# A product in the element order of the transpose that follows it, and a rewritten task order

## The chip, the core and the metric

The kernel runs on one core of a Trainium2 chip. The core has five instruction streams that run beside each other and wait for one another by semaphores: PE (TensorE, matrix products into PSUM), ACT (ScalarE), DVE (VectorE), POOL (GpSimd) and SP (SyncE, which here only issues transfers). The metric is the device time of one execution in microseconds; the median of the runs counts.

## The reference

The input x has 2048 positions and 640 channels. A conditioning vector c gives six modulation vectors. The first half of the block multiplies a shifted k with v, convolves the product along the whole sequence with a filter as long as the sequence, and multiplies by q. The second half is a two-layer MLP with a shift of channel groups between.

```python
mod = (silu(c) @ w_mod)                    # sa, ca, ga, sb, cb, gb
h = layernorm(x) * (1 + ca) + sa           # this is q of the first half
k_shift = sum(k_pad[:, t:t+S, :] * shift_k[:, ks-1-t] for t in range(4))
kv = k_shift * v
y = irfft(rfft(kv, 2*S) * rfft(ssm_k, 2*S))[:S] + kv * ssm_D
x = x + ga * (h * y)
h = layernorm(x) * (1 + cb) + sb
m = gelu(layernorm(h) @ w1)                # four channel groups shifted by 1, -1, 2, -2 positions
x1 = h + shift(m) @ w2
x = x + gb * (x1 + gelu(layernorm(x1) @ w3) @ w4)
```

Everything is bfloat16 outside of the accumulations.

## The kernel before

The Fourier transforms are products with cosine and sine matrices that the kernel makes itself. A position is n = 64 * n2 + n1, and a transform has two stages: stage 1 over n2 (32 values), stage 2 over n1 (64 values).

The channels are taken in five blocks of 128 partitions, b = 0 to 4. `sT`, `kT` and `vT` hold the filter, k and v with channels on partitions and positions along the free dimension; `dma_start_transpose` brings k and v in so. `kT` and `vT` share the buffer R5. For each block, `k_shift(b, s2)` makes half of the shifted k (1024 positions) with eight matmuls against diagonal matrices into a PSUM tile `ps_ksh` (line 457), and DVE multiplies the tile with v (line 462). `to_slots` (line 395) then lets DVE transpose the 2048 bf16 numbers of a partition as 1024 pairs (seen as int32) in squares of 32 by 32, into `kvL`, which is Rb. Its result has n2 on the partitions, which is what stage 1 contracts over. The filter goes the same way (`sL`, also in Rb, from Ra). `stage1` (line 408) puts its result into T01 through evacuations of PSUM by ACT (line 209) or DVE (line 211), and `stage2` (line 425) puts the spectra into R3 (filter, `KSX`) and R5 (product, `XS`, over kT and vT). Stage 2 takes its matrices `Gs` from RG. `inverse1` multiplies the spectra on DVE (line 606) and transforms back (lines 617 and 618), `inverse2` (line 658) finishes.

RH holds two of the three buffers for the early pieces of w_mod and after them the matrices of `inverse2`.

The MLP follows in sixteen tiles of 128 positions, in groups g: three single tiles first, then pairs. `chain_a` (lines 734 and 737) adds the first half to x, `chain_b` (748 or 752, then 753) modulates, `chain_c` (721 or 583) normalizes and turns the tile for the products `mm_w1` (815, 825), `mm_w2` (870), `mm_w3` (904) and `mm_w4` (934). Each chain ends in a layer norm: ACT squares and sums (726), `ln_finish` takes the mean on POOL or DVE (699 to 704) and the power -1/2 on POOL (709 to 714). `ln1_stats` (528 on DVE, or 536 and 537 on ACT) and `ln1_fin` (546 to 551, POOL) do the same for the first layer norm, which `make_q` (583 or 581, 590, 591) applies.

The order of the work is written out by hand in the string `ORDER`. Every call of `add` makes a numbered task with its reads and writes. A word of `ORDER` such as `121D` puts task 121 into the queue of DVE at that place; P is PE, A is ACT, G is POOL, S is SP, and the digits after a colon are the places (of four) in PSUM. A queue runs in this order, and a task waits there for its inputs. Some tasks may be given to either of two engines. The tasks that the text names:

| tasks | what |
|---|---|
| 32, 33; 45, 46 to 48 | negation of a part of Gs, and copies of it, first and second half |
| 116 to 135 | k_shift: matmuls (even) and product (odd), four to a block |
| 460 to 471 | first layer norm's statistics for tiles 8 to 15; 463 is tile 10, 464 tile 11, 467 tile 13 |
| 498, 502 to 511 | inverse2 for tiles 3 to 15 |
| 519, 520, 521, 522, 523 | tile 0, chain_a: two on DVE, the square, the mean, the power |
| 524, 525, 526, 527, 528, 529 | tile 0, chain_b and the normalization 529 |
| 540 to 549, 550 | tile 1, the same (543 and 544 end chain_a, 548 and 549 end chain_b) |
| 560 to 569, 570 | tile 2 |
| 588 to 595 | tiles 3 and 4, chain_a (594 and 595 end it) |
| 580, 581, 582 | first mm_w2, its sum and its square |

Of the kernel before, what the change touches and what calls it, by code (L numbers as in the profile page):

```python
# [10 lines left out]
I32 = mybir.dt.int32  # L11
ACT = mybir.ActivationFunctionType
ALU = mybir.AluOpType
PSUM = bass.MemoryType.PSUM

S, D, F = 2048, 640, 1728
P = 128
NT = S // P
ND = D // P
# [4 lines left out]
LFFT = 4096  # L24

ORDER = """
0S 19G 18D 20D 2S 27G 28D 31A 29D 30A 21G 23D 22D 4S 36G 37G 68G 69D 24A 25A 26G 84P:0 85A 3S 86P:1 87A 90P:2 91A 50G 72G 52D 73D 106P:3 107A 102P:0
104P:1 70G 71D 96P:2 6S 5S 88P:3 103D 74D 75D 8S 49G 118P:0 9S 119D 38G 105A 97A 39G 40A 89A 98P:1 99A 114P:2 1S 66D 10S 108P:3 115D 109A 92P:0 32G
67D 41G 93A 42G 43G 44A 54A 116P:1 11S 51D 53A 94P:2 112P:3 113A 117D 7S 122P:0 123D 80P:1 110P:3 111D 95A 81A 76P:2 77A 100P:0 101D 78P:1 82P:3 79A
33S 253D 34S 120P:2 121D 45G 46G 83A 178P:0 55G 179A 47S 184P:1 185A 35S 140P:3 141A 190P:0 191D 146P:1 147A 142P:2 143D 174P:3 175A 170P:0 182P:1  # L30
183A 171D 136P:2 137A 56G 200S 194P:3 144P:0 145A 195D 168P:1 48S 162P:2 163A 169D 148P:3 149D 192P:0 193A 196P:1 172P:2 173A 160P:3 161A 12S 57G 58G
197D 188P:0 189D 156P:1 152P:2 150P:3 176P:0 157A 151A 153D 177D 164P:1 138P:2 139D 165A 154P:3 155A 186P:0 187D 254D 158P:1 159A 180P:2 181A 260P:3
166P:0 167D 59G 60A 61G 201S 198P:1 261A 62G 63G 199D 124P:2 268P:3 203S 202S 211A 269A 13S 125D 14S 208A 65G 210D 15S 126P:0 266P:1 16S 270P:2 271A
128P:3 127D 264P:0 267A 265A 262P:2 263A 213D 214A 17S 130P:1 255D 276P:0 277A 129D 209D 219S 258P:2 259A 131D 134P:3 274P:0 275A 280P:1 281A 64A 135D
363G 278P:2 279A 132P:3 272P:0 273A 212G 220P:1 221A 256D 282P:2 283A 133D 222S 223P:3 224A 257D 288P:0 289A 284P:1 285D 292P:2 293A 286P:3 225S
294P:0 295A 290P:1 287D 291D 296P:2 297A 226P:3 227D 228S 229P:0 340P:1 230D 322P:2 231S 323D 341A 348P:3 349A 234S 480D 232P:0 249G 233D 326P:1 327A
243S 238S 360P:2 361D 356P:3 357A 328P:0 314P:1 250G 315A 358P:2 359A 329D 336P:3 306P:0 307A 318P:1 337D 320P:2 321A 319D 237G 483D 244S 330P:3 331A
352P:0 353D 242S 354P:1 355A 235P:2 386S 300P:3 236D 310P:0 311D 301A 246G 308P:1 239G 316P:2 317D 324P:3 309A 240S 350P:0 332P:1 312P:2 325A 251S
333A 313A 351D 298P:3 299D 247G 304P:0 305A 252G 344P:1 345D 241S 302P:2 303A 245G 338P:3 339D 342P:0 343A 334P:1 335D 346P:2 347A 364D 362S 365D
368P:3 486A 487D 369A 488D 248G 366P:0 216A 372D 370S 371G 367A 373D 374P:1 375A 376P:2 387G 481D 378S 377A 379G 380D 381D 442S 443P:3 382P:0 384P:1  # L40
385A 389D 388D 392P:2 394S 383A 393A 390P:1 391A 395G 397D 396D 398P:0 399A 402S 400P:2 401A 403G 405D 410S 411G 404D 408P:1 409A 406P:0 407A 413D
412D 416P:2 417A 420D 414P:1 415A 489A 418S 419G 421D 422P:0 423A 424P:2 425A 448S 449P:1 426S 427G 428D 450A 429D 430P:0 431A 432P:2 433A 436D 435G
434S 437D 438P:1 439A 440P:0 441A 490D 457S 458P:2 459A 454S 484D 444D 455P:3 479G 445S 456A 215G 495P:10 497A 217D 451S 452P:2 482D 492D 491D 218G
493D 453A 446P:3 485D 494D 496D 519D 532A 498P:01 499A 500A 501G 447D 511P:23 520D 522G 521A 513A 540D 560D 512A 541D 472S 502P:01 478G 505P:32 561D
524D 562A 473S 542A 591D 523G 525D 204S 526A 592D 593A 503A 504A 533D 588D 507A 563G 564G 543G 527D 565D 589D 590A 528G 529D 530P:0 531A 508P:12 566D
567A 545D 544G 546D 476S 477S 594G 595G 568D 548D 547A 535P:0 206S 553D 510A 600D 509A 596D 601D 597D 506A 536A 549G 550D 205S 602D 603A 551P:2 474S
537P:1 538A 475S 569G 570D 552D 571P:3 598D 534D 604G 572D 207S 599A 605G 558P:0 559A 556P:2 557A 554D 651D 578P:1 579A 555D 652D 576P:3 577A 653A
654D 609D 606D 607P:0 655D 656A 516S 467A 464D 610P:2 611D 580P:1 608D 620P:3 581D 582A 618P:2 621A 619A 657G 658G 663D 664D 665D 666A 659D 583G 584G
585D 586P:0 660D 661D 662A 514S 667D 587A 622P:1 461D 668G 669D 463A 623D 670S 625P:3 518G 636P:2 637A 671D 672S 624A 638P:0 639A 460D 462G 626D 627A
640P:1 641A 628D 629G 633D 630D 681P:2 682A 679P:3 680A 634P:0 642P:1 465G 643A 676D 677D 631P:2 635A 469D 632D 615A 616D 686P:3 687D 683P:1 617D 684D  # L50
466A 678D 703P:0 689G 515S 573A 697P:2 688A 699P:3 685A 704A 574D 575D 719D 690G 673D 720D 698A 785D 694A 695P:1 691D 692P:0 612A 693A 613D 614D 722D
721A 517S 644P:2 723D 700A 696A 724A 725G 769P:0 674D 765P:3 675D 786D 788D 789D 791D 645D 726G 727A 787A 701P:1 728D 766A 731D 729D 646D 770A 763P:2
468G 732D 733D 790A 702A 705P:30 730A 734A 792G 793D 647S 797D 735G 767P:1 851D 744A 852D 736G 739D 740S 741A 794D 706P 795D 798D 799D 796A 707D 801G
737A 738S 749P:3 800A 764A 802G 805D 806S 853A 747P:2 768A 708D 750A 803D 748A 804S 815P:1 816A 813P:3 713D 814A 754P:0 742D 711S 751P:2 743D 854D
855D 755D 714D 857G 817P:1 756A 752D 757D 856A 858G 863D 864D 865D 650S 753A 758G 712S 761D 759D 745D 648S 866A 859A 771P:30 773D 860D 861D 862A 709S
762S 820P:2 821D 772P 649S 774D 760S 835P:3 818D 867G 715S 868G 836A 871D 872S 470A 716S 822A 831P:2 832A 869D 870S 829P:1 875P:3 873P:2 819A 876A
833P:3 823D 824G 825D 826S 827A 471G 779D 810D 874A 877P:0 539G 811D 807D 828S 830A 878D 880P:2 710S 881D 895P:1 879A 893P:0 882A 894A 889P:2 834A
883G 884G 887D 885A 886S 746D 780D 888S 911D 778S 891P:0 812D 890A 912D 913A 808D 809D 914D 915D 916A 917D 775S 892A 896A 837P:32 897P:01 839D 717S
718S 840D 971D 972D 781S 841S 777S 973A 899D 918G 923A 955P:3 953P:0 838P 924D 844S 974D 925D 898P 783S 975G 919D 920D 921D 976D 922A 927D 926A 977D
978D 928G 929A 845D 776S 980D 979A 981G 956A 842S 930S 982A 949P:2 931D 932S 935P:3 954A 936A 784S 933P:0 934A 782S 983S 984P:3 985A 986P:0 987A 846D  # L60
905D 848S 988G 937P:1 843S 938D 939A 940P:3 941D 942A 906D 943G 951P:0 952A 989P:1 992P:3 950A 993D 990D 995D 1023P:0 957P:23 944G 947A 900D 948S 945A
959D 946S 991A 1007P:1 1008A 1005P:2 1001P:1 1024D 1025A 994A 996G 999A 997A 901S 958P 1002A 965D 1003P:0 1026G 1027G 998S 1000S 1030P:1 1004A 1036P:3
1037A 1031A 1034P:0 910S 1006A 1028D 1029S 1058P:3 1009P:12 1062D 849S 1063D 907S 1035A 1032P:0 850S 847S 960D 1011D 963S 1052P:1 1033A 909S 903S
1010P 1053A 1059A 1054P:0 1038P:13 904S 902S 966D 970S 967S 962S 1017D 961S 968S 908S 964S 1018D 1020S 1012D 1040D 1056P:2 1016S 1039P 1015S 969S
1041D 1044S 1043S 1013S 1022S 1046D 1014S 1047D 1042S 1045S 1021S 1055A 1019S 1057A 1060P:01 1064D 1049S 1065D 1050S 1048S 1067S 1051S 1069S 1061P
1070D 1071D 1073A 1066S 1068S 1075A 1074S 1072S
"""


# [69 lines left out]
def kernel(  # L139
# [4 lines left out]
    nc = tc.nc  # L144
# [11 lines left out]
    add = pl.add  # L156
# [4 lines left out]
    Rb = mem.tile([P, 10240], BF, name="Rb")  # L161
# [4 lines left out]
    RH = mem.tile([P, 4096], BF, name="RH")  # L166
# [12 lines left out]
    kvL = Rb  # L179
    x_all = Ra[:].rearrange("p (a d) -> p a d", d=D)  # L180
    kT = R5[:, 0:10320].rearrange("p (b n) -> p b n", b=ND)
# [18 lines left out]
    def cd(n):  # L200
        return 0.14 + 0.00104 * n
# [135 lines left out]
    for kb in range(2):  # L337
# [9 lines left out]
        else:  # L347
# [3 lines left out]
            r=[wk[:3]], w=[wk], port=0.4)  # L351
# [37 lines left out]
    add("POOL", 3.7, f, r=[("ccol", 0, 1)], w=[("siluc", 0, 1)])  # L389


    def to_slots(dst, dkey, src_b, skeys, b):
        o = dst[:, 2048 * b:2048 * (b + 1)].bitcast(I32).rearrange("p (r j) -> p j r", r=32)
        i = src_b.bitcast(I32).rearrange("p (n j) -> p j n", n=32)
        add("DVE", 2.02, lambda e: nc.vector.transpose(out=o, in_=i), r=skeys, w=[(dkey, 2048 * b, 2048 * b + 2048)])  # L395

    F1r = F1bd[:].rearrange("p q c k -> p (q c k)")
# [48 lines left out]
            stage1(sL, "Rb", b, h, "s")  # L446


    def k_shift(b, s2):
        ps = Slot()  # L450

# [7 lines left out]

        def f(e):  # L460
            vs = vT[:, b, 1024 * s2:1024 * s2 + 1024]
            nc.vector.tensor_tensor(vs, ps.tile[:].rearrange("p i n -> p (i n)"), vs, ALU.mult)
        t1 = add("DVE", cd(1024), f, w=[("vT", b, b + 1, "f")], use=ps)
        dep(t1, t0)

    for b in range(ND):
        for s2 in range(2):
            k_shift(b, s2)
    stage2(KSX, "R3")


# [94 lines left out]
            dma(("SP", "POOL"), 64, lambda q, js=js, jd=jd: q.dma_start(RH[32 * jd:32 * jd + 32, 1024 * js:1024 * js + 1024], RK[32 * js:32 * js + 32, 3072:4096]),  # L566
                r=[("RK", 3072, 4096)], w=[("RH", 1024 * js, 1024 * js + 1024, "h")], rate=215.0)

    for b in range(ND):
        to_slots(kvL, "Rb", vT[:, b, :], [("vT", b, b + 1)], b)  # L570
    for b in range(ND):
        for h in range(2):
            stage1(kvL, "Rb", b, h, "kv")
# [488 lines left out]
```

## Time and profile before

| | |
|---|---|
| median of 6 runs | 309.08 us (308.36 to 310.68) |
| profiled execution, its own time | 309.01 us |
| its span, first to last instruction | 307.0 us |
| busy: PE, DVE, ACT, POOL | 272.2, 219.0, 210.1, 115.9 us |
| mean granted TensorE clock | 0.957 |

A busy time is the sum of an engine's instructions; PE's is modelled from pipelined matmuls and does not say that PE works at its peak. In the groups, `out<-in` names the tiles, then come shapes and types, the count, the busy time, the mean of one in ns, and the idle time just ahead of them with what ended it. In a timeline the first two numbers are start and duration in us, and brackets hold the idle time before.

### The profile page before, as it was taken

Reading aid. Unit: us, or ns where it says so; the run is one execution under the profiler, and the core shown is the slowest. Engines: PE = TensorE matmul, PEld = TensorE weight load, DVE = VectorE, ACT = ScalarE, POOL = GpSimd, SP = SyncE. Lnnn points to the kernel's source line nnn. Section 1 sums busy time; section 2 is a strip of 40 time slices with the busy share of each in tenths; the row PEclk is TensorE's granted clock in tenths of the full one; section 3 lists DMA queues with packets and bytes.
Section 4 is the critical chain, followed back from the end, with each engine's and each line's share of the span. In section 5 each row is a group of like instructions: output and inputs, shape, how many; then the busy total and the mean of one; then the engine's idle time right before and its main releaser. Section 6 shows DMA issues by size and latency. Waiting matters only on the chain.

```text
span 307.0 us, 7413 instructions
## 1 busy us (share of the span) xinstructions
PE 272.2 (89%) x2922; PEld 206.2 (67%) x2926; DVE 219.0 (71%) x430; ACT 210.1 (68%) x359; POOL 115.9 (38%) x257
## 2 busy tenths in 40 slices
PE   0999999996999856668999989999999899999992
PEld 0655555753988644656788767688867777887761
DVE  8999999999899998888689773925759135032342
ACT  4889999987779788998896686376643673642200
POOL 5898085061223688643337521424113130300000
PEclk9999999999699965799999999999999999999998
DMA  6999999579799922602800340222420402151112
GB/s 206 267 195 215 212 179 224 162 194 234 214 257 334 264 62 58 246 2 43 288 7 0 24 79 19 53 50 48 40 62 2 88 2 48 22 71 34 43 47 59
DMA packets 58163, 35.74 MB, mean 116 GB/s; under 512 B 39872, under 2 KB 54848, under 8 KB 58128
## 3 DMA queue, kind: packets, MB, share of 16 engines
q1 hardware_dynamic: 56896, 31.81, 44.3%
q0 software_dynamic: 1136, 3.41, 3.9%
q8 instruction: 23, 0.38, 0.5%
q14 instruction: 12, 0.10, 0.1%
q10 hardware_dynamic: 96, 0.04, 0.1%
HBM read 16.31 MB, written 2.62 MB: 62 GB/s over the span
## 4 chain that ended last, share of the span: by engine, by line
PE 52%; POOL 13%; DMA 10%; ACT 9%; DVE 9%; issue 4%; SPq 1%; POOLq 0%; ACTq 0%; DVEq 0%
PE ps_w L934 13%; PE ps_w L904 13%; PE ps_s L425 5%; PE ps_w L870 4%; DMA RG<-in_B_w_dram 4%; POOL lnv L712 4%; PE ps_w L815 4%; PE ps_ksh L457 3%; DMA R<-RK 3%; PE ps_s L408 3%; ACT R L209 2%; DVE Rb L606 2%; DMA Ra<-in_A_ssm_k_dram 2%; ACT RG L726 2%; PE ps_i L618 2%
## 5 line engine op out<-in xcount | busy, mean ns | idle before, releaser
L904 PE MATMUL ps_w<-R,T 128*128 128x256 bf16 (+1 forms) x630 | 64.0, 261 | 0.0
L904 PEld LDWEIGHTS <-T 128*128 128x128 bf16 x630 | 55.8, 98 | 7.4 <-issue 1.1
L934 PE MATMUL ps_w<-T,R 128*128 128x320 bf16 x416 | 59.0, 299 | 0.0
L934 PEld LDWEIGHTS <-R 128*128 128x128 bf16 x416 | 40.3, 98 | 15.4 <-issue 0.3
L908 ACT ACTIVATE R<-ps_w 128x1024 bf16<-128x1024 f32 (+2 forms) x36 | 28.9, 826 | 28.6 <-PE ps_w L904 28.5
L726 ACT ACTIVATE RG<-R 128x640 bf16<-128x640 bf16 x32 | 23.5, 734 | 18.9 <-DVE R L753 10.6
L209 ACT CAST T<-ps_s 128x1024 bf16<-128x1024 f32 x33 | 31.4, 1026 | 2.7 <-PE ps_s L408 2.7
L957 DVE TENSOR_TENSOR T<-ps_w,R 128x640 bf16<-128x640 f32 x15 | 12.3, 823 | 28.6 <-PE ps_w L934 16.7
L408 PE MATMUL ps_s<-F1bd,Rb 128*128 128x256 bf16 x160 | 22.0, 286 | 9.0 <-DVE Rb L395 8.1
L408 PEld LDWEIGHTS <-Rb 128*128 128x128 bf16 x160 | 16.0, 102 | 15.1 <-DVE Rb L395 8.7
L877 DVE SCALAR_TENSOR_TENSOR R<-ps_w,R 128x640 bf16<-128x640 f32 x16 | 13.0, 818 | 17.8 <-PE ps_w L870 14.7
L209 ACT CAST R<-ps_s 128x640 bf16<-128x640 f32 x37 | 23.4, 725 | 1.9 <-PE ps_s L425 1.8
L617 PE MATMUL ps_i<-EA,Rb 128*128 128x128 bf16 x160 | 21.9, 236 | 3.1 <-DVE Rb L606 2.7
L712 POOL TENSOR_TENSOR lnv<-lnv,mhalf 128x2 f32<-128x2 f32 (+1 forms) x29 | 22.5, 777 | 2.3
L209 ACT CAST T<-ps_i 128x1024 bf16<-128x1024 f32 x20 | 19.1, 1021 | 5.8 <-PE ps_i L618 5.8
L870 PE MATMUL ps_w<-RG,R 128*128 128x320 bf16 x160 | 23.1, 299 | 0.0
L618 PE MATMUL ps_i<-EB,Rb 128*128 128x128 bf16 x160 | 21.8, 236 | 1.2 <-DVE Rb L606 1.2
L425 PE MATMUL ps_s<-T,RG 64*128 64x320 bf16 x256 | 22.0, 297 | 0.6 <-ACT R L209 0.3
L211 DVE CAST R<-ps_s 128x640 bf16<-128x640 f32 x27 | 20.7, 818 | 1.0 <-ACT R L209 0.3
L815 PE MATMUL ps_w<-R,RG 128*128 128x256 bf16 (+1 forms) x200 | 20.5, 264 | 0.0
L617 PEld LDWEIGHTS <-Rb 128*128 128x128 bf16 x160 | 17.0, 107 | 4.1 <-DVE Rb L606 4.0
L711 POOL TENSOR_TENSOR lnv<-stat,lnv 128x2 f32<-128x2 f32 x19 | 5.5, 292 | 37.0 <-ACT RG L726 36.5
(173 smaller groups left out, 523.6 us busy)
## 6 DMA issues: line engine op xcount, KB each, us to landing
Ra<-in_A_ssm_k_dram SPq DMA_DIRECT2D x5, 512.0 KB, 5.2
Ra<-in_A_q_dram SPq DMA_DIRECT2D x8, 320.0 KB, 5.6
R<-in_w_mod_dram SPq DMA_DIRECT2D x6, 400.0 KB, 6.7
out_dram<-RH SPq DMA_DIRECT2D x60, 40.0 KB, 1.6
T<-in_B_w_dram SPq DMA_DIRECT2D x1, 2160.0 KB, 10.4
T<-in_B_w_dram SPq DMA_DIRECT2D x1, 2080.0 KB, 10.2
RH<-in_w_mod_dram SPq DMA_DIRECT2D x4, 400.0 KB, 4.9
RK<-R POOLq DMA_DIRECT2D x5, 256.0 KB, 5.5
```

Source lines behind the costliest of these rows:

```text
L209: nc.scalar.copy(dst, src(ps.tile))
L408: nc.tensor.matmul(psv[:, ml, :], lhsT=xL[:, s0:s0 + P], rhs=F1r, start=True, stop=True)
L425: nc.tensor.matmul(psv[:, g], lhsT=Gs[p, k, 64 - 64 * cc:192 - 64 * cc], rhs=T1b[p, cc * 32 + k], start=(cc == 0), stop=(cc == 1), tile_po ...
L617: nc.tensor.matmul(psv[:, w, :], lhsT=Av[:, r_, :, g_], rhs=EAf, start=True, stop=False)
L618: nc.tensor.matmul(psv[:, w, :], lhsT=Bv[:, r_, :, g_], rhs=EBf, start=False, stop=True)
L712: nc.gpsimd.tensor_tensor(rs, rs, mhalf[:, 0:n], ALU.pow)
L726: add("ACT", 0.74, lambda e: nc.scalar.activation(junk, src, ACT.Square, scale=float(D) ** -0.5, accum_out=stat[:, li, 1, t:t + 1]), r=[sk ...
L815: nc.tensor.matmul(pt[:, fb, 0:cw], lhsT=w1_sb[:, b, 160 * fb:160 * fb + P], rhs=hT[:, b, 0:cw], start=(b == 0), stop=(b == ND - 1))
L870: nc.tensor.matmul(pt[:, hf, 0:320], lhsT=gsf[:, fb, c0:c0 + P], rhs=w2_sb[:, fb, 320 * hf:320 * hf + 320], start=(fb == 0), stop=(fb == 4))
L904: nc.tensor.matmul(pt[:, fl, 0:cw], lhsT=w3_sb[:, b, fb * P:(fb + 1) * P], rhs=xT[:, b, 0:cw], start=(b == 0), stop=(b == ND - 1))
L908: nc.scalar.activation(g3[g % 2][:, f0:f0 + fn, 0:cw], ps.tile[:, 0:fn, 0:cw], ACT.Gelu_apprx_tanh)
L934: nc.tensor.matmul(bank(i, hf), lhsT=gg[:, fb, i * P:(i + 1) * P], rhs=w4_sb[:, fb, 320 * hf:320 * hf + 320], start=(fb == 0 and i == 0), ...
```

## The change

The product is no longer written over v. It goes into `kvp[b]`: for block 0 the first 2048 columns of RH, for block b above 0 the k block b-1, whose matmuls are over by then. It is written so that the pairs stand in the order in which the transpose reads them (`flat`): a position pair (n, j), n of 32 and j of 32, is at j * 32 + n and no longer at n * 32 + j. The transpose writes as before. The transpose of block 0 is made ahead of stage 2 of the filter in the program text, so that tasks 136 to 252 move up by one number and the old 253 is 136. The whole of `ORDER` is replaced; old numbers in it are shifted accordingly. The lines of it that matter here:

```diff
 ORDER = """
...
-33S 253D 34S 120P:2 121D 45G 46G 83A 178P:0 55G 179A 47S 184P:1 185A 35S 140P:3 141A 190P:0 191D 146P:1 147A 142P:2 143D 174P:3 175A 170P:0 182P:1
...
-493D 453A 446P:3 485D 494D 496D 519D 532A 498P:01 499A 500A 501G 447D 511P:23 520D 522G 521A 513A 540D 560D 512A 541D 472S 502P:01 478G 505P:32 561D
...
-567A 545D 544G 546D 476S 477S 594G 595G 568D 548D 547A 535P:0 206S 553D 510A 600D 509A 596D 601D 597D 506A 536A 549G 550D 205S 602D 603A 551P:2 474S
-537P:1 538A 475S 569G 570D 552D 571P:3 598D 534D 604G 572D 207S 599A 605G 558P:0 559A 556P:2 557A 554D 651D 578P:1 579A 555D 652D 576P:3 577A 653A
-654D 609D 606D 607P:0 655D 656A 516S 467A 464D 610P:2 611D 580P:1 608D 620P:3 581D 582A 618P:2 621A 619A 657G 658G 663D 664D 665D 666A 659D 583G 584G
...
+10S 112P:2 94P:0 122P:3 67D 32G 41G 42G 43G 51D 44A 45D 117D 54A 53A 95A 113A 80P:0 81A 11S 123D 110P:1 111D 76P:2 77A 7S 100P:3 101D 82P:0 83A 78P:1
...
+497A 519D 452P:0 453A 446P:3 447D 219G 501G 520D 522G 540D 521A 560D 541D 475S 511P:12 524D 561D 472S 478G 513A 532A 533D 553D 523G 498P:03 499A 500A
+591D 588D 525D 534D 527D 592D 542A 589D 512A 543G 545D 544G 563G 565D 502P:20 504A 562A 564G 526A 477S 528G 529D 503A 594D 566D 590A 546D 505P:31 476S
...
+537P:3 538A 552D 598D 599A 652D 604D 605G 571P:1 208S 572D 554D 555D 558P:0 559A 606D 609D 473S 654D 655D 556P:2 557A 578P:3 579A 474S 576P:1 577A
+610P:0 611D 207S 464D 607P:2 608D 514S 653A 657G 656A 658G 580P:3 581D 582A 620P:1 621A 659D 618P:0 619A 663D 664D 583G 584G 665D 585D 660D 666A
...
+462G 615D 467A 612D 613D 616D 704A 697P:2 688A 689G 614D 685A 690G 691D 692P:0 700A 694A 695P:1 721A 693D 701P:3 702A 696D 769P:0 765P:1 516S 698A
...
@@ -389,9 +389,10 @@
     add("POOL", 3.7, f, r=[("ccol", 0, 1)], w=[("siluc", 0, 1)])
 
 
-    def to_slots(dst, dkey, src_b, skeys, b):
+    def to_slots(dst, dkey, src_b, skeys, b, flat=False):
         o = dst[:, 2048 * b:2048 * (b + 1)].bitcast(I32).rearrange("p (r j) -> p j r", r=32)
-        i = src_b.bitcast(I32).rearrange("p (n j) -> p j n", n=32)
+        i = src_b.bitcast(I32)
+        i = i.rearrange("p (j n) -> p j n", n=32) if flat else i.rearrange("p (n j) -> p j n", n=32)
         add("DVE", 2.02, lambda e: nc.vector.transpose(out=o, in_=i), r=skeys, w=[(dkey, 2048 * b, 2048 * b + 2048)])
 
     F1r = F1bd[:].rearrange("p q c k -> p (q c k)")
@@ -446,6 +447,9 @@
             stage1(sL, "Rb", b, h, "s")
 
 
+    kvp = [RH[:, 0:2048]] + [kT[:, b, 16:16 + S] for b in range(ND - 1)]
+    kvk = [("RH", 0, 2048)] + [("kT", b, b + 1) for b in range(ND - 1)]
+
     def k_shift(b, s2):
         ps = Slot()
 
@@ -459,13 +463,16 @@
 
         def f(e):
             vs = vT[:, b, 1024 * s2:1024 * s2 + 1024]
-            nc.vector.tensor_tensor(vs, ps.tile[:].rearrange("p i n -> p (i n)"), vs, ALU.mult)
-        t1 = add("DVE", cd(1024), f, w=[("vT", b, b + 1, "f")], use=ps)
+            nc.vector.tensor_tensor(kvp[b].rearrange("p (j n x) -> p n j x", n=32, x=2)[:, 16 * s2:16 * s2 + 16],
+                                    ps.tile[:].rearrange("p i (n j x) -> p (i n) j x", j=32, x=2),
+                                    vs.rearrange("p (n j x) -> p n j x", j=32, x=2), ALU.mult)
+        t1 = add("DVE", cd(1024), f, r=[("vT", b, b + 1)], w=[kvk[b] + ("f",)], use=ps)
         dep(t1, t0)
 
     for b in range(ND):
         for s2 in range(2):
             k_shift(b, s2)
+    to_slots(kvL, "Rb", kvp[0], [kvk[0]], 0, True)
     stage2(KSX, "R3")
 
 
@@ -566,8 +573,8 @@
             dma(("SP", "POOL"), 64, lambda q, js=js, jd=jd: q.dma_start(RH[32 * jd:32 * jd + 32, 1024 * js:1024 * js + 1024], RK[32 * js:32 * js + 32, 3072:4096]),
                 r=[("RK", 3072, 4096)], w=[("RH", 1024 * js, 1024 * js + 1024, "h")], rate=215.0)
 
-    for b in range(ND):
-        to_slots(kvL, "Rb", vT[:, b, :], [("vT", b, b + 1)], b)
+    for b in range(1, ND):
+        to_slots(kvL, "Rb", kvp[b], [kvk[b]], b, True)
     for b in range(ND):
         for h in range(2):
             stage1(kvL, "Rb", b, h, "kv")
```

Between the two orders 46 tasks change their engine. Those that the text names: 45 and 594 go from POOL to DVE, 33 from SP to POOL, and among the copies into RH one goes from SP to POOL and two from POOL to SP. In the warm-up of the MLP POOL's queue was 523, 563, 564, 543, 528, 544, 594, 595, 549, 569 and becomes 523, 543, 544, 563, 564, 528, 595, 549, 569.

## The prediction

> **What bounds the kernel now.** I read the busy time by stage first, because the share of the whole span mixes stages with different limits. The columns are the stretch in us from the span's start, its length, the busy time of PE, weight loads, DVE, ACT and POOL with instruction counts, the granted TensorE clock, the DMA share and GB/s.
>
> ```profile
> 25.00:58.00 33.00, 32.05 (x259) 19.22 (x260) 32.16 (x37) 32.21 (x51) 15.99 (x27) 1.00 0.99 200
> 110.00:126.00 16.00, 9.49 (x312) 7.40 (x313) 13.55 (x34) 14.48 (x26) 13.44 (x23) 0.50 0.33 111
> 126.00:150.00 24.00, 18.85 (x226) 16.26 (x224) 18.44 (x52) 21.24 (x55) 11.98 (x32) 0.97 0.31 93
> 150.00:303.00 153.00, 149.73 (x1276) 117.06 (x1273) 81.76 (x196) 81.96 (x150) 36.35 (x103) 1.00 0.23 45
> ```
>
> From 25 to 58 us, where the change works, PE, DVE and ACT are all about 97% busy: none can gain much before another stops it. From 150 us on PE is idle 3.3 us in 153, so the end is where PE's full stretch begins plus a fixed 153 us and the drain; whatever moves the start of that stretch moves the end one for one. Between lies the warm-up of the MLP pipeline, 110 to 150 us, where PE is idle 6.5 + 5.2 us, at half clock at first, and the layer norms go through POOL, ACT and DVE. So three places matter: the forward transform, the first layer norms, the stretch to 150 us.
>
> Next the groups by form, for the operations that change:
>
> ```profile
> L211 DVE CAST R<-ps_s 128x640 bf16<-128x640 f32 x27 | 20.7, 818 | 1.0 <-ACT R L209 0.3 <-PE ps_s L425 0.2
> L462 DVE TENSOR_TENSOR R<-ps_ksh,R 128x1024 bf16<-128x1024 f32 x10 | 11.9, 1200 | 0.2 <-PE ps_ksh L457 0.2
> L395 DVE STREAM_TRANSPOSE Rb<-Ra 128x1024 int32<-128x1024 int32 x5 | 10.2, 2073 | 0.0
> L395 DVE STREAM_TRANSPOSE Rb<-R 128x1024 int32<-128x1024 int32 x5 | 9.9, 1979 | 0.0
> L211 DVE CAST T<-ps_s 128x1024 bf16<-128x1024 f32 x7 | 8.4, 1216 | 0.1
> ```
>
> The five transposes of k*v are the second L395 row, 1.98 us each; the ten products are L462, 1.20 us each. Two casts of different length give DVE's rate from PSUM: (1216 - 818) / 384 = 1.036 ns per element and 155 ns fixed, so 1024 elements at one per step take 1.22 us. The transpose takes 0.76 us more than that.
>
> The chain that ended last, at the end of this stage:
>
> ```profile
> 54.15 1.24 DVE R L462
> 55.41 2.00 DVE Rb L395
> 57.45 2.36 PE ps_s L408 x20
> ```
>
> The last product and the last transpose are on the chain. But PE fills this time with other blocks and module weights and its wait for that transpose is only 0.23 us. Last, the warm-up, engine by engine (POOL, then ACT with one DVE row, then PE):
>
> ```profile
> 111.32 0.71 POOL L712 TENSOR_TENSOR lnv<-lnv,mhalf 128x1 f32<-128x1 f32 x1
> 112.12 0.92 POOL L699 TENSOR_SCALAR lnv<-stat 128x1 f32<-128x1 f32 x1
> 115.28 0.42 POOL L699 TENSOR_SCALAR lnv<-stat 128x1 f32<-128x1 f32 x1
> 116.48 0.19 POOL L709 TENSOR_TENSOR lnv<-stat,lnv 128x1 f32<-128x1 f32 x1
> 118.29 0.40 POOL L699 TENSOR_SCALAR lnv<-stat 128x2 f32<-128x2 f32 x1
> 121.66 0.19 POOL L709 TENSOR_TENSOR lnv<-stat,lnv 128x1 f32<-128x1 f32 x1
> ```
>
> ```profile
> 133.34 0.74 ACT L536 ACTIVATE RG<-Ra 128x640 bf16<-128x640 bf16 x1
> 134.20 0.74 ACT L537 ACTIVATE RG<-Ra 128x640 bf16<-128x640 bf16 x1
> 135.06 0.74 ACT L726 ACTIVATE RG<-R 128x640 bf16<-128x640 bf16 x1
> ```
>
> ```profile
> 133.76 0.81 DVE L877 SCALAR_TENSOR_TENSOR R<-ps_w,R 128x640 bf16<-128x640 f32 x1
> ```
>
> ```profile
> 123.76 0.71 PE L769 MATMUL ps_tr<-RG,RK 128*128 128x128 bf16 x5 [1.38 <-DVE RK L721]
> 131.36 0.73 PE L769 MATMUL ps_tr<-RG,RK 128*128 128x128 bf16 x10 [1.89 <-DVE RK L583]
> ```
>
> POOL works without a gap from 109 to 125 us, in the written order 523, 563, 564, 543, 528, 544, 594, 595, 549, 569. PE waits behind it at 117.85 (tile 0), 123.76 (tile 1) and 125.38 us (tile 2). At 133.34 ACT takes early statistics of a late tile (two passes and two accumulator reads, 1.7 us) while the L877 sum that the next square needs is complete at 134.58: that square starts at 135.06.
>
> **The change, part by part.** The profiled execution took 309.01 us (span 307.0 and 2.0 around it), 0.07 under the median of 309.08; the sum is made on 309.0.
>
> *The transposes' read side.* They now read consecutive words; their writes still step 32 words (128 bytes) each element. No row has that mix. The ends are 1.22 us (one element per step) and 1.98 us (nothing gained); a loss is excluded as far as reading in order is part of every faster row. The nearest row is the present one, which shares the write side. Here the Trainium skill speaks against the change: "Vector Engine (DVE) Microarchitecture Reference", section 5.2, measures 1.71 ns per column where only the destination hops each element and 1.98 where both sources and the destination do, and says that the penalties "only partly add". The row now is (1979 - 155) / 1024 = 1.78 ns per element. By the rule with the fixed part of the rows a transpose becomes 0.155 + 1.71 x 1.024 = 1.91 us, an estimate: 0.07 saved, 0.35 us in all five. With the read side as the whole cost it would be 3.8 us. I take 1.91.
>
> *The product's write side.* It writes two bf16 (4 bytes) and hops 128 bytes. The same section asks for runs of two adjacent 4-byte words for the full rate; taken strictly each product would be 0.155 + 1.71 x 1.024 = 1.91 instead of 1.20 us, 7 us more on DVE. But the L211 row R<-ps_s writes exactly such 4-byte pairs 128 bytes apart, at 818 ns, and L877 writes the same number densely at 818 in its group. The row decides: 0, bounds 0 to +0.7 each. A gain is excluded, since 1.20 is already the rate of a PSUM read.
>
> *What reaches the end.* DVE loses 0.35 us of 32.2. ACT has 0.8 us idle in those 33 us and PE 0.95, and almost every evacuation stays on its engine until the second transform, so at most 0.8 us of any DVE saving comes through there. After it, ACT makes 17 evacuations in a row to 74.4 us. I count 0.1 us; bounds 0 and 2.1 (ACT's 0.8 and its 1.3 idle from 58 to 74.4).
>
> *Buffers and waits.* The product of block b goes into k block b-1, whose matmuls precede it on PE in the order; block 0 goes into RH, which the first module weights enter only at 47.5 us, over 20 us after the first transpose (25.5 us). The product still waits for its own matmul and v load. Cost 0; if RH were late, the two weight loads of SP would stand before all later loads of that queue, and the mod matmuls at 54.4 us come some 2 us after those loads land.
>
> *The rewritten order, queues.* The Gs negation (task 45) goes from POOL (1.5 us at 20.27) to DVE, about 0.45 us by L583's bf16 row of 448 ns. POOL gains nothing that is on the chain, which left it at 20.3; DVE pays up to 0.45 in a stage with 0.1 us idle, but PE's second stage only needs it after 27 us: 0, bounds -0.4 to +0.4. Gs copy 33 moves from SP to POOL (an issue of 0.8 us like the one at 22.07); three of the RH copies change queue; the first KSY copy (362) and one late x load move ahead in SP. The transfers are covered: inverse transform 1 starts on DVE's first multiply at 74.42, released by ACT, not by a copy. The small w2 loads go in front of w1 and the big one behind: w1 landed at 103.4 and PE uses it at 120, w2 landed near 108 and is used at 131.9. Cost 0; past these covers it would cost all of the lateness.
>
> *First layer norms.* POOL's order becomes 523, 543, 544, 563, 564, 528, 595, 549, 569, with 594 on DVE. By the present durations 543 + 544 + 563 + 564 take 112.1 to 117.3 and 528 ends near 118.2 rather than 117.3: tile 0 is 0.9 us later. Without 594's 1.5 us POOL is free for 549 and 569 earlier, but DVE puts 529 (which waits for 528) in front of 594, 566 and 546, so 546 ends about 120.7 and 549 starts at 121.7 as before. Only 569 gains, 0.5 to 1.4 us. PE's wait of 1.38 before tile 1 disappears behind the later first W1 group (2.3 us). I count -0.4; bounds -1.5 and +0.9.
>
> *To 150 us.* The statistics of tile 13 (467) leave ACT's queue ahead of the square (582), which can start at 134.6: -0.5. Tile 10's (463) move behind too, but at 140.5 the chain runs over POOL and DVE, 0. Several norms go from ACT to DVE (0.92 to 0.45 us each), and ACT is the busiest engine here, 21.2 of 24: counted 0, bound -1.0.
>
> Sum: 309.0 - 0.1 - 0.4 - 0.5 = 308.0; I put a small part, 0.1, of the ACT relief with it: **307.9 us**. A measurement of this kernel can tell about 0.5%, 1.5 us, from no change.
>
> **The rivals.**
>
> *Read side was the whole cost.* Transposes at 1.22 us, 3.8 us off DVE, at most 2.1 through ACT's gaps: 309.0 - 2.1 - 0.9 = 306.0. For it: the row from Ra (2073) is longer where loads arrive, so memory access counts. Against: the write side is untouched, and the section above.
>
> *Nothing comes through.* Transposes stay at 1.98 and the order's gains stop at PE's in-order waits for DMA transposes (1.69 us at 146.14): 309.1.
>
> *Slower: tile 0 holds the queue.* 528 is sixth in POOL; DVE's 529 waits for it with 594, 566 and 546 behind. If 528 ends after about 118.2, its 0.9 us goes on to the following groups and g3's 595 waits for 594 once more, about 1.0: 309.0 + 1.9 = 310.9. It decides from there on, because PE's slack before tile 1 is only 1.38 us. Against: POOL loses 1.5 us of work.
>
> *Slower: the product hops.* At 1.91 us each DVE has 7.1 - 0.4 = 6.7 more; 0.8 is idle, about 4.7 would reach the end with the products outside the busiest stretch left out: 313.7. It decides from a product of about 1.3 us. Against: the L211 row.
>
> **How the numbers follow.** The counted case has chance 0.46 with about 1.3 us either way: faster 0.19, no change 0.25, slower 0.02. The read-side case 0.19, all faster. Nothing through 0.10: 0.01, 0.08, 0.01. Tile 0 0.17 and the product 0.08, all slower. Together faster 0.39, within 0.5% 0.33, slower 0.28. The likeliest case alone is 306.6 to 309.2; the range of 305.0 to 311.5 leaves out the product case and the tails of the read-side and tile-0 cases, some 0.2.
>
> **What would show it.** Right: L395 from R or RH between 1.83 and 1.98 us, L462 within 1.25; ACT and PE still about 97% busy from 25 to 58; inverse transform 1 starting within 0.4 us of 74.4; the first W1 group 0.5 to 1 us later than 120.07, but the 1.38 us wait before tile 1 gone; no L536 ahead of the L726 near 135; PE's full stretch from about 149. Wrong: a transpose near 1.22 with the second transform ending over 1 us earlier; a product above 1.3 us; a first W1 group past 122 us with 150 us reached late.

## The result, and the profile after

The changed kernel takes 307.75 us (median of 36 runs, 306.4 to 309.27), the kernel before 309.23 us beside it (73 runs): ratio 0.9944, interval 0.9931 to 0.9956, so 1.7 us faster by the ratio. The profiled execution took 308.08 us with a span of 306.2 us (before: 309.01 and 307.0). In the new numbering most lines are one to seven higher: the transpose is L396, the product L466, stage 1 L409.

The same stretches as before the change, in the same columns:

```profile
25.00:58.00 33.00, 32.12 (x259) 19.43 (x260) 31.99 (x37) 32.11 (x50) 15.94 (x27) 1.00 1.00 209
110.00:126.00 16.00, 9.08 (x323) 6.58 (x322) 14.46 (x40) 14.10 (x26) 12.93 (x21) 0.57 0.25 59
126.00:150.00 24.00, 19.19 (x207) 16.25 (x207) 16.32 (x47) 20.19 (x51) 7.26 (x21) 0.93 0.53 181
150.00:303.00 153.00, 151.11 (x1299) 118.55 (x1297) 87.38 (x205) 82.61 (x152) 41.81 (x119) 1.00 0.18 39
```

From 25 to 58 us, where the element order works, nothing moved: PE 32.05 to 32.12, DVE 32.16 to 31.99, ACT 32.21 to 32.11. The stretch that did move is the last one: PE's idle time from 150 to 303 us fell from 3.27 to 1.89 us. That is the stretch that the prediction had called fixed.

The groups by form, transposes and products now split by the buffer of the product:

```profile
L211 DVE CAST R<-ps_s 128x640 bf16<-128x640 f32 x27 | 20.7, 817 | 1.3 <-PE ps_s L426 0.9
L396 DVE STREAM_TRANSPOSE Rb<-Ra 128x1024 int32<-128x1024 int32 x5 | 10.3, 2079 | 0.3 <-POOL Ra L442 0.3
L466 DVE TENSOR_TENSOR R<-ps_ksh,R 128x1024 bf16<-128x1024 f32 x8 | 9.7, 1211 | 0.2
L396 DVE STREAM_TRANSPOSE Rb<-R 128x1024 int32<-128x1024 int32 x4 | 7.8, 1962 | 0.0
L466 DVE TENSOR_TENSOR RH<-ps_ksh,R 128x1024 bf16<-128x1024 f32 x2 | 2.4, 1210 | 0.0
L396 DVE STREAM_TRANSPOSE Rb<-RH 128x1024 int32<-128x1024 int32 x1 | 2.0, 1969 | 0.0
```

A transpose with a consecutive source takes 1.96 us, 0.02 us less than before. A product that hops takes 1.21 us, 0.01 more. Over five transposes and ten products the two cancel.

The chain at the end of this stage used to hold the last product and the last transpose. It no longer does; ACT's evacuations of PSUM stand there, and the last product of stage 1 begins 1.4 us later (60.9 us in place of 59.5):

```profile
55.23 1.82 ACT T L209 x2
57.05 0.33 ACT modv L505
57.38 0.92 ACT T L209
58.30 0.35 ACT modv L505
58.64 0.92 ACT T L209
59.57 0.04 issue
59.61 1.58 PE ps_s L409 x12
```

The warm-up, POOL, then ACT, then PE (brackets: idle time before, and what ended it):

```profile
118.01 1.09 POOL L719 TENSOR_TENSOR lnv<-lnv,mhalf 128x1 f32<-128x1 f32 x1
...
119.34 0.54 POOL L719 TENSOR_TENSOR lnv<-lnv,mhalf 128x1 f32<-128x1 f32 x1
121.06 0.62 POOL L718 TENSOR_TENSOR lnv<-stat,lnv 128x2 f32<-128x2 f32 x1 [1.18 <-ACT RG L733]
...
133.74 0.73 ACT L733 ACTIVATE RG<-Ra 128x640 bf16<-128x640 bf16 x1
134.59 0.74 ACT L733 ACTIVATE RG<-Ra 128x640 bf16<-128x640 bf16 x1
...
125.30 0.45 PE L776 MATMUL ps_tr<-RG,RK 128*128 128x128 bf16 x5 [0.38 <-DVE RK L728]
132.71 0.73 PE L776 MATMUL ps_tr<-RG,RK 128*128 128x128 bf16 x10 [0.15 <-DVE RK L590]
147.74 0.71 PE L832 MATMUL ps_w1x<-R,RG 128*128 128x256 bf16 x5 [0.51 <-DMA R<-RK]
185.16 0.71 PE L832 MATMUL ps_w1x<-R,RG 128*128 128x256 bf16 x5 [0.40 <-DMA R<-RK]
```

POOL now has a gap, ACT makes its squares without the early statistics in between, and these waits of PE are shorter: 1.38 us is 0.38, 1.89 is 0.15, 1.69 is 0.51. Others have come in their place (1.12 us at 127.98, 0.92 at 142.37), and PE's idle time from 110 to 150 us is 11.7 us in both kernels. The kernel before also waited 0.96 us at 184.00, which is 0.40 now, and 0.85 us at 242.24, which has no counterpart now.

When each stage begins (us), with four of the experiments below. W1 and W4 are the products `mm_w1` and `mm_w4`. The last two columns are differences: from the start of the first W1 product to the start of the last W4 product, and from there to the end of the span.

| kernel | inverse 1 | inverse 2 | first W1 | last W4 begins | W1 to W4 | W4 to end |
|---|---|---|---|---|---|---|
| before | 74.4 | 102.8 | 120.1 | 301.1 | 181.0 | 5.9 |
| after | 75.7 | 104.4 | 122.6 | 301.0 | 178.4 | 5.2 |
| e2, element order only | 75.2 | 102.8 | 120.0 | 301.4 | 181.4 | 6.9 |
| e6, new from inverse 1 | 74.8 | 102.6 | 120.8 | 299.4 | 178.6 | 5.4 |
| e7, new from 168 us | 74.8 | 102.2 | 119.4 | 299.1 | 179.7 | 4.9 |
| e8, new up to 180 us | 75.4 | 102.8 | 121.5 | 301.8 | 180.3 | 6.1 |

The changed kernel reaches its first W1 product 2.5 us late and yet begins its last W4 product at the same time.

### The profile page after: what moved, and what is told of

It reads as the page before. It is cut to its first block, busy times and chain, and to the rows that moved or that the text cites. A ratio compares the mean times of both kernels' runs of the same rounds, so it can differ in the third digit from the quotient of the medians.

```text
span 306.2 us, 7408 instructions
## 1 busy us (share of the span) xinstructions
PE 272.9 (89%) x2922; PEld 207.1 (68%) x2926; DVE 222.3 (73%) x437; ACT 207.6 (68%) x355; POOL 112.4 (37%) x257
## 4 chain that ended last, share of the span: by engine, by line
PE 57%; ACT 13%; DMA 9%; POOL 7%; DVE 7%; issue 4%; SPq 0%; DVEq 0%; ACTq 0%; POOLq 0%
PE ps_w L911 20%; PE ps_w L941 18%; PE ps_w L877 6%; ACT T L209 5%; PE ps_w L822 3%; PE ps_s L426 3%; ACT R L209 3%; DMA RG<-RG 3%; DVE Rb L613 3%; DMA Ra<-in_A_ssm_k_dram 2%; DMA RK<-R 2%; DMA R<-RK 2%; POOL lnv L719 1%; PE ps_i L625 1%; ACT RG L733 1%
## 5 line engine op out<-in xcount | busy, mean ns | idle before, releaser
L409 PE MATMUL ps_s<-F1bd,Rb 128*128 128x256 bf16 x160 | 22.2, 289 | 9.8 <-POOL Ra L442 8.5
L409 PEld LDWEIGHTS <-Rb 128*128 128x128 bf16 x160 | 16.3, 104 | 15.7 <-DVE Rb L396 8.7
L719 POOL TENSOR_TENSOR lnv<-lnv,mhalf 128x2 f32<-128x2 f32 (+1 forms) x29 | 21.2, 732 | 2.3
L211 DVE CAST R<-ps_s 128x640 bf16<-128x640 f32 x27 | 20.7, 817 | 1.3 <-PE ps_s L426 0.9
L822 PE MATMUL ps_w<-R,RG 128*128 128x256 bf16 (+1 forms) x200 | 21.5, 273 | 0.0
L838 ACT ACTIVATE R<-ps_w1x 32x256 bf16<-32x256 f32 (+1 forms) x40 | 13.2, 330 | 10.6 <-PE ps_w1x L832 10.2
L822 PEld LDWEIGHTS <-RG 128*128 128x128 bf16 x200 | 18.6, 110 | 1.6 <-issue 0.2
```

The source lines that it names most:

```text
L409: nc.tensor.matmul(psv[:, ml, :], lhsT=xL[:, s0:s0 + P], rhs=F1r, start=True, stop=True)
L719: nc.gpsimd.tensor_tensor(rs, rs, mhalf[:, 0:n], ALU.pow)
L822: nc.tensor.matmul(pt[:, fb, 0:cw], lhsT=w1_sb[:, b, 160 * fb:160 * fb + P], rhs=hT[:, b, 0:cw], start=(b == 0), stop=(b == ND - 1))
```

## The experiments

The theory after the result was that the element order is worth nothing and the task order makes the whole gain; the rivals were that the element order does it, and then, in turn, each stretch of the order. Each kernel was timed beside the kernel before on the same chip. Three chips were used, one for e1 to e4, one for e5 to e8 and one for e9 to e12, and the kernel before took 309.36, 309.65 and 311.16 us on them, so the kernels are compared by their ratios to it. e11 and e12 have one execution each and are read from their traces. A kernel that changes over from one order to the other does it ahead of the task named; its diff shows the first words on either side of that place.

**e1: the new order with the old product and transposes.** Its only edit to the kernel before is the string `ORDER`, in the old numbers:

```diff
-0S 19G 18D 20D 2S 27G 28D 31A
+19G 18D 2S 27G 21G 20D 29D 30A
...
```

> The product in place over v as before, with the changed kernel's task order (its numbers mapped back). Theory A (all of the gain is the order; the element order is worth nothing because the transpose is held by its writes): 1.3 to 1.7 us faster than before, the same as the changed kernel; k*v transposes 1.98 us, products 1.20. Theory B (the read order brings the gain): no gain, 309.2.

Measured 307.7 beside 309.36, ratio 0.994 (0.992 to 0.9959): the ratio of the full change.

**e2: the element order with the old task order.** The changed kernel with:

```diff
-19G 18D 2S 27G 21G 20D 29D 30A
+0S 19G 18D 20D 2S 27G 28D 31A
...
```

> The product in the transposes' order into the dead k blocks, with the task order of before (its numbers mapped). Theory A: within 0.3 us of before; k*v transposes 1.95 to 1.98 us, products 1.20 to 1.22. Theory B: 1.3 to 1.7 us faster than before.

Measured 309.39 beside 309.36, ratio 0.9994 (0.9976 to 1.0012). Together: the element order is worth nothing that these runs can tell (about 0.5 us either way), and the order of the tasks has the gain of 1.7 us.

**e3 and e4: the order by halves, cut at task 495 near 100 us.** e3 has the old forward and first inverse transform and the new order behind; e4 the reverse. e3 and e4 against the changed kernel:

```diff
-19G 18D 2S 27G 21G 20D
+0S 19G 18D 20D 2S 27G
...
-495P:21 218D 459A 482D
+495P:21 218D 482D 451S
```

```diff
-495P:21 218D 459A 482D
+495P:10 497A 218D 451S
...
```

> The changed kernel, with the order of before up to the last stage of the inverse transform (task 495) and the new order from there on. If the gain lies in the MLP's warm-up, steady part or tail: 1.2 to 1.8 us faster than before. If it lies in the forward transforms: 0 to 0.3 us faster.

> The changed kernel, with the new order up to task 495 and the order of before from there on. If the gain lies in the MLP: between 0.3 us faster and 1 us slower than before, since in the profile inverse transform 1 began 1.3 us later than before (75.7 for 74.4), which may have been the loads of that one run. If it lies in the forward transforms: 1.2 us or more faster.

Measured 309.4 (0.9997, interval 0.9974 to 1.0019) and 309.48 (1.0004, 0.9986 to 1.0023): neither half shows the gain. For e4 that stands. e3 can mislead, because the cut made a mixture that neither order has: a load of x (task 205) comes ahead of a load of w_mod on SP. That this brings the loss is not shown. In its trace the second inverse transform loses time that the others don't, with a wait for which the profile shows no cause:

```profile
115.86 2.10 PE L665 MATMUL ps_i<-T,RH 32*32 32x160 bf16 x128 [5.06 <-issue]
```

The same row has 1.52 in the kernel before, 1.58 in the changed one and at most 2.99 in any other trace. The first W1 came 21.2 us behind the start of inverse 2, and 16.6 to 18.7 us in the other timed kernels. From its first W1 product to the end of the span e3 takes 183.8 us, as the changed kernel does (183.6, before 186.9): in its trace the gain is there, and lost ahead of it. So its time decides nothing, and later cuts were put where both orders have done nearly the same tasks up to there.

**e5: the two words of SP swapped back.** The changed order issues the first filter block (2S) ahead of the tiny load of ssm_D (0S). e5 is the changed kernel with:

```diff
-19G 18D 2S 27G
+19G 18D 0S 27G
...
-37G 0S 68G
+37G 2S 68G
```

> The changed kernel with one edit: the tiny load of ssm_D (task 0) again ahead of the first filter block (task 2) in SP's queue. If this swap is why inverse transform 1 began 1.3 us later after the change: first transpose at about 5.8 us again, inverse transform 1 at 74.6 to 75.0, and, since PE is full behind the warm-up, 0.5 to 1.1 us faster than the changed kernel (306.7 to 307.3). If the old warm-up's slack is what swallowed such a shift before: no difference, 307.7.

Measured 306.44 beside 309.65, ratio 0.9916 (0.9884 to 0.9948). In the trace of the changed kernel POOL is held by ssm_D at its add to the filter; in that of e5 it waits for the filter block alone and starts 0.6 us earlier:

```profile
6.17 0.19 POOL L442 TENSOR_TENSOR Ra<-Ra,Dcol 128x1 bf16<-128x1 bf16 x1 [2.44 <-DMA Dcol<-in_A_ssm_D_dram]
```

```profile
5.56 0.24 POOL L442 TENSOR_TENSOR Ra<-Ra,Dcol 128x1 bf16<-128x1 bf16 x1 [1.83 <-DMA Ra<-in_A_ssm_k_dram]
```

From issue to landing the tiny load took 4.6 to 5.1 us in the six kernels that issue it behind the block, and 2.9 to 3.4 in the others. Inverse 1 starts at 75.4 to 76.1 us in five of the six and at 74.4 to 75.4 with the old start, but once, in e10, at 76.7 with the old start and a slow first block. So the wait is shown. Its price is not settled: inverse 1 starts 1.1 us earlier in e5 than in the changed kernel, but traces with the same start differ by up to 1.0 us, and the intervals of the two ratios overlap.

**e6 and e7: the new order only from later on.** e6 keeps the old order up to task 364, where inverse 1 begins; e7 up to task 813, near 168 us. Both against the changed kernel:

```diff
-19G 18D 2S 27G 21G 20D
+0S 19G 18D 20D 2S 27G
...
 364D 365D 368P:0 369A
```

```diff
-19G 18D 2S 27G 21G 20D
+0S 19G 18D 20D 2S 27G
...
 813P:3 711S 754P:0 751P:1
```

> The changed kernel with the order of before up to the first multiply of inverse transform 1 (task 364) and the new order from there on. If the seam of the third kernel (a tile load of SP put in front of a module weight load, PE idle 5.1 us without a wait at 111) was what took its gain: now 1.3 to 2.5 us faster than before, 307.0 to 308.0. If the new MLP order needs the new forward order: no gain, 309.2.

> The changed kernel with the order of before up to task 813 (some 168 us) and the new order from there on. Of PE's waits in the profiles, those at 184 and 242 us fall from 1.8 to 0.4, and the tail ends 0.7 us sooner: if these are independent of the warm-up, 1.0 to 2.0 us faster than before; if the gain is made in the warm-up to 150 us, at most 0.7 faster.

Measured 307.49 (0.9939, 0.9911 to 0.9967) and 306.13 beside 309.65 (0.9894, 0.9858 to 0.993, from 6 runs). e7 has the lowest ratio of all: it keeps the whole gain, so the gain lies behind 168 us. It is 1.5 us below the changed kernel by the ratios, while its interval only just clears that one's, so the new start and warm-up bring nothing and probably take something back. In the table above the new warm-up shortens W1 to W4 by about 1 us (e6 against e7) and delays the first W1 by as much (18.2 us behind inverse 2 in e6, 17.2 in e7). Of the two waits that e7 was expected to shorten only the one near 242 us is gone; the one at 184 us is still 0.92 us, and 0.38 to 0.40 in every kernel with the new warm-up.

**e8: the new order only up to 180 us.** The complement of e7, cut at task 829 (the changed kernel with the old order behind):

```diff
-829P:1 870S 875P:0 650S
+829P:1 875P:3 873P:2 876A
...
```

> The changed kernel with the new order up to task 829 (some 175 to 180 us) and the order of before from there on: the complement. If the gain is made behind it: no gain over before, up to 1 us slower. If it is made in the warm-up: 1 to 1.7 us faster than before.

Measured 308.97 beside 309.65, ratio 0.9994 (0.9969 to 1.0018): start and warm-up of the new order alone bring nothing. PE's wait near 242 us is back:

```profile
242.93 0.71 PE L832 MATMUL ps_w1x<-R,RG 128*128 128x256 bf16 x5 [1.17 <-DMA R<-RK]
```

**e9 and e10: the last words apart from the middle.** e9 has the new order only behind task 1060 (the last products), e10 only from task 813 to 1060. e9, then e10, against the changed kernel:

```diff
-19G 18D 2S 27G 21G 20D
+0S 19G 18D 20D 2S 27G
...
 1060P:32 1061P 1064D 1065D
```

```diff
-19G 18D 2S 27G 21G 20D
+0S 19G 18D 20D 2S 27G
...
 813P:3 711S 754P:0 751P:1
...
-1060P:32 1061P 1064D 1065D
+1060P:01 1064D 1065D 1048S
```

> The code of the changed kernel with the old order up to task 1060 (the last group's products) and the new order only for the words behind it. The kernel before issues five transfers on SP after the last DVE operation (2.28 us) and its L981 row waited 1.09 us for an out_dram transfer; the changed kernel issues three (1.35 us) and has no such wait. Theory A, the tail is a gain of its own: 0.5 to 1.1 us faster than the kernel before (308.4 to 309.0 beside 309.5), with three SP issues behind the last DVE row. Theory B, the tail only follows from where the middle's transfers stand in SP's queue: no change (ratio 1.000, within 0.2%) and as many issues at the end as before.

> The code of the changed kernel with the old order up to task 813, the new order from there to task 1060 (about 168 to 300 us), and the old order again behind that. The kernel with the new order from 168 us to the end was 306.1 beside 309.65. Theory A, the middle makes most of the gain by ending PE's wait for a DMA transpose near 242 us: 1.0 to 2.5 us faster than the kernel before, no PE wait near 242, and a tail as long as before's. Theory B, the tail makes all of it: no change, and the PE wait near 242 may go without moving the end.

Measured 310.65 and 307.6 beside 311.16: ratios 1.0007 (0.9975 to 1.0038) and 0.9907 (0.988 to 0.9934). The middle has the whole gain, and the last words don't bring it. This cut makes a mixture as well, with a wait of PE at the last group's products that no other kernel has; in e9:

```profile
299.15 1.93 PE L941 MATMUL ps_w<-T,R 128*128 128x320 bf16 x13 [0.92 <-DVE T L964]
```

Both orders put the last two groups into PSUM so that task 1060 takes over the place that DVE reads first; at the cut it takes over the one that DVE reads last. e10 has the same wait, also 0.92 us, so its gain stands in spite of it. In e9 it could hide a gain of the last words of up to about 0.9 us, and that stays open.

I had read the shorter tail of the changed kernel (three issues in SP's last row, where the kernel before has five) as a gain of its own. The number of issues does not make it: e10 has six there and the shortest end of all, 4.5 us behind the start of its last W4 product, and e9 has three, and 5.6 us. So the shorter end comes with the middle, which is not what theory A of e10 expected. SP's last row in e10:

```profile
302.31 2.89 SPq L991 DMA_DIRECT2D out_dram<-RH  x6
```

**What the middle does.** e10 says where, the two traces say how. The kernel before works on the last tiles like this (DVE, ACT, SP, PE):

```profile
226.42 0.49 DVE L963 TENSOR_TENSOR RH<-T,Ra 128x640 bf16<-128x640 bf16 x1 [0.29 <-DMA out_dram<-RH]
226.83 0.48 DVE L734 TENSOR_TENSOR R<-Rb,RQ 128x640 bf16<-128x640 bf16 x1
227.42 0.83 DVE L737 SCALAR_TENSOR_TENSOR Ra<-R,Ra 128x640 bf16<-128x640 bf16 x1
...
228.35 0.74 ACT L726 ACTIVATE RG<-Ra 128x640 bf16<-128x640 bf16 x1 [3.88 <-DVE Ra L737]
229.09 0.91 ACT L581 ACTIVATE R<-Ra,lnv 128x640 bf16<-128x640 bf16 x1
...
237.69 3.04 SPq L762 DMA_TRANSPOSE R<-RK  x2
240.77 1.03 SPq L966 DMA_DIRECT2D out_dram<-RH  x2
241.92 1.20 SPq L762 DMA_TRANSPOSE R<-RK  x1
...
242.24 0.71 PE L825 MATMUL ps_w1x<-R,RG 128*128 128x256 bf16 x5 [0.85 <-DMA R<-RK]
```

and the changed kernel:

```profile
222.00 0.83 DVE L744 SCALAR_TENSOR_TENSOR Ra<-R,Ra 128x640 bf16<-128x640 bf16 x1
226.44 0.79 DVE L590 TENSOR_SCALAR R<-Ra,lnv 128x640 bf16<-128x640 bf16 x2
...
224.43 0.74 ACT L733 ACTIVATE RG<-Ra 128x640 bf16<-128x640 bf16 x1
...
234.24 4.01 SPq L769 DMA_TRANSPOSE R<-RK  x3
```

The products that wait at 242.24 belong to tiles 13 and 14, the last pair, and the delay reaches them through tile 15. On DVE, chain_a of tile 15 (971 and 972) used to stand behind an output of an earlier group (839 and 840), which first waits for PE and then for a transfer out of RH; now it follows 911 and 912 directly. Its sum is done 5.4 us earlier and its square on ACT 3.9 us. Behind that square ACT used to normalize tile 14 (task 923, the row at 229.09); now DVE does this together with tile 13 at 226.44. The first transposes into R begin 3.5 us earlier, and PE no longer waits for them. e10's trace has the same: its three transposes begin at 235.12 in place of e9's 238.09 on the same chip, and e9's wait of 1.08 us at 242.98 is absent. Over all fourteen traces the wait is there (0.77 to 1.29 us) in the five with the old words in the middle and absent in the nine with the new ones. Of e10's gain of 2.9 us by its ratio, this wait is about 1 us and the shorter end about 1 us; the remainder I can't assign. Which of these moves does it, the two words of tile 15 or task 923's change of engine, was not tried.

**e11: transposes with both sides consecutive.** One line of the changed kernel:

```diff
-        o = dst[:, 2048 * b:2048 * (b + 1)].bitcast(I32).rearrange("p (r j) -> p j r", r=32)
+        o = dst[:, 2048 * b:2048 * (b + 1)].bitcast(I32).rearrange("p (j r) -> p j r", r=32)
```

> The changed kernel whose transposes (line 396) write consecutive words as well; the transposed layout, and so what is computed behind it, is not the reference's. It is a measurement of one operation. Theory A, the write side's hop is the whole cost above one element per step: the k*v transposes (both sides dense) fall from 1.96 to about 1.22 us and the filter's (source hopping, destination dense) to about 1.22 as well. Theory B, either hop alone is enough: the filter's stay at 1.96 to 2.07 and only the k*v ones fall to 1.22. Theory C, a transpose of squares has a price of its own whatever the pattern: both stay near 1.96.

The groups of its DVE operations:

```profile
L396 DVE STREAM_TRANSPOSE Rb<-Ra 128x1024 int32<-128x1024 int32 x5 | 9.7, 1948 | 0.2 <-POOL Ra L442 0.2
L396 DVE STREAM_TRANSPOSE Rb<-R 128x1024 int32<-128x1024 int32 x4 | 4.9, 1227 | 0.0
```

With the rows of the other kernels every combination is there: both sides hop 1.98 us (from Ra 2.07), only the write 1.96, only the read (from Ra) 1.95, neither 1.23. Theory B holds: either hop alone costs nearly all of the 0.75 us, so mending one side is worth 0.02 us, or 0.13 where the source is Ra. One more thing is read from this run. Its transposes of k*v are 3.7 us shorter in sum (five times 0.73), and from 25 to 58 us DVE is busy 29.05 us in place of 31.99, while PE and ACT stay within 0.4 us of what they were:

```profile
25.00:58.00 33.00, 31.92 (x260) 19.18 (x259) 29.05 (x37) 31.77 (x50) 15.92 (x27) 1.00 1.00 211
```

Inverse 1 starts at 76.1 us, no sooner than the 75.4 to 75.7 of the other kernels with the same start: in this trace DVE time saved here does not reach the next stage. The one time, 307.6 us on a chip where the kernel before takes 311.16, is too little to settle it at the end.

**e12: the product written one bf16 at a time.** One line of the changed kernel:

```diff
-            nc.vector.tensor_tensor(kvp[b].rearrange("p (j n x) -> p n j x", n=32, x=2)[:, 16 * s2:16 * s2 + 16],
+            nc.vector.tensor_tensor(kvp[b].rearrange("p (x j n) -> p n j x", n=32, x=2)[:, 16 * s2:16 * s2 + 16],
```

> The changed kernel whose product (line 466) writes every bf16 singly, at 64-byte distance, instead of pairs of two at 128-byte distance; the element order and so what is computed behind it is not the reference's. It is a measurement of one operation. Theory A, the write pattern costs DVE nothing as long as one source is in PSUM: L466 stays at 1.20 to 1.22 us. Theory B, it is the pair that keeps the rate: single elements cost [...]about 1.9 us each, 7 us more on DVE between 25 and 66 us, and the kernel is about 2 to 5 us slower than the changed one.

(More exactly than the expectation has it: successive elements go by turns to two halves 2048 bytes apart, and each half steps by 64 bytes.)

```profile
L466 DVE TENSOR_TENSOR R<-ps_ksh,R 128x1024 bf16<-128x1024 f32 x8 | 35.8, 4562 | 2.3 <-PE ps_ksh L461 2.3
```

A product takes 4.55 us in place of 1.21, (4562 - 155) / 1024 = 4.30 ns per element, well above theory B's 1.9 us, which is the prediction's estimate for a product that hops. By the means of the groups the ten of them cost DVE 33.4 us more, and inverse 1 starts at 110.3 us, 34.5 behind that of the changed kernel (the one time is 341.9 us): all of it gets through. So the pair is what makes the change harmless.

## Why the prediction came out as it did

The time, 307.9 us against 307.75 measured, was near, but not by its own reasons, and so by luck: of the 1.1 us of gain in its sum (1.7 measured, by the ratio) it placed 1.0 in the warm-up, which turned out to bring nothing, and the real gain lies where it counted 0.

- **Transposes, read side** (counted 1.91 from 1.98): measured 1.96. The direction of the argument was right, that the write side's hop remains, and the size was small either way. The Trainium skill ("Vector Engine (DVE) Microarchitecture Reference", section 5.2), with 1.71 for a hopping destination and 1.98 for all three ports, left 0.07 us for the read side; it is worth 0.02. Its 1.71 is for hops of 4 KiB and a two-source operation, and for steps of 24 words, nearer to the 32 words here, the same table has 2.50, which the prediction passed over. The measured row, (1962 - 155) / 1024 = 1.76 ns, lies close to the first. "Only partly add" is here nearly "don't add".
- **Product, write side** (counted 0): right, 1.21 against 1.20. The L211 row with its 4-byte pairs decided it well; the same section's demand for two adjacent 4-byte words, from which the prediction worked out 1.91, does not hold for this row of bf16 pairs. The rival *the product hops* is refuted, and e12 shows that its mechanism exists one step further on.
- **What reaches the end** (counted 0.1 of 0.35): not tested by the change, since transposes and products together saved nothing. In e11 nothing of a larger saving is seen at inverse 1. The rival *read side was the whole cost* at 306.0 is wrong twice: the transposes didn't shorten, and in e11, where they did, inverse 1 came no sooner.
- **Buffers and waits** (counted 0): nothing in e2 speaks against it.
- **Queues** (counted 0): the first step that failed. The prediction followed the copies, the w2 loads and POOL's moved task through SP's and POOL's queue, and passed over the first three words of the order, where a load of 640 numbers changes places with a filter block. Inverse 1 began at 75.7 us, not within 0.4 of 74.4. That POOL waits for ssm_D is shown (0.6 us between the two rows above); what it costs at inverse 1 is not settled. Without e10 and e12, the means of the traces with the new and the old start differ by 0.8 us.
- **First layer norms and to 150 us** (counted -0.4 and -0.5): the second that failed. The named waits did shrink (1.38 to 0.38, 1.89 to 0.15), the square no longer has statistics ahead of it, and tile 0 is later by about the 0.9 us that was named: POOL ends task 528 at 119.88 us, 15.5 us behind the start of inverse 2 and not 14.5, and the first W1 comes 18.2 us behind it and not 17.2. But the two cancel: e7, without the new warm-up, is 306.13, and e6, with it, 307.49 (their intervals overlap). Shorter waits were counted as gain where others took their place. The wait of 1.89 us was a poor witness besides: under the same old order it is 1.14 in e7, 0.60 in e9 and 0.65 in e10. The sign that was named as wrong, a first W1 past 122 us, did come, in part through the later start of inverse 2.
- **PE's full stretch as a fixed 153 us** (counted 0): the third, and the one that hid the gain. The 3.3 us of idle time in it was taken as small; it was the largest thing to be had. Its waits at 184 and 242 us are for DMA transposes, and PE runs in order, so each pushes what is behind it. The one at 242 us ended with the new middle; the one at 184 us shrank with the new warm-up and is no part of the middle's gain (0.92 us in e7 and 0.93 in e10). The fixed drain was wrong as well, by 0.7 us.
- The rival *tile 0 holds the queue* is right that tile 0 comes later by 0.9 us and wrong that it is carried to the end: the following groups waited less. The rival *nothing comes through* describes the new start and warm-up as they turned out (e8: 0.9994), though not for its reason, since the wait of 1.69 us at 146.14 that it named is 0.50 in e8; of the whole order it is wrong.

## What to carry to other kernels

Where three engines are about 97% busy in one stretch, a saving on one of them may bring nothing (3.7 us of DVE in e11, none of it seen at the next stage) while an excess comes through (33 us in e12). When a diff replaces a written order, read it stretch by stretch to its end, and in a stretch that one engine fills, look first at its few remaining waits: in an in-order queue each of them can be time of the kernel, and the word to move may be on another engine, several operations upstream. Split such a diff by running old words up to a place and new ones behind it, and look at the place of the cut in the trace, since it can make a mixture that costs by itself (0.92 us in e9 and e10).

## What the hardware showed that I had not expected

- A transpose of 1024 int32 per partition in 32 by 32 squares takes 1.95 to 1.96 us if one side hops 128 bytes at each element, 1.98 to 2.07 if both do, and 1.23 us if neither does: the two hops hardly add.
- Pairs of bf16 at 128-byte distance are written as fast as consecutive ones by a product with one source in PSUM (1.21 and 1.20 us for 1024). Single bf16, by turns to two places 2048 bytes apart, took 4.30 ns per element, 4.55 us.
- The tiny load of ssm_D landed 4.6 to 5.1 us after its issue when a filter block was issued ahead of it on the same queue, and 2.9 to 3.4 us when it was first.
- In inverse 2, where PE has hundreds of small products, its waits for nothing that the profile shows differ between traces for one and the same row of 128 products: 0.75 to 2.99 us, and 5.06 us once, in e3. The cause stays open.
